# Decay attention and softplus feed-forward: scores of four jobs of batch 0 in two one-pass products, with a new plan

## The chip, the cores and the metric

The kernel runs on one core of one Trainium2 chip. The metric is the device time of one execution in microseconds, median of three. A profile of one execution shows what each engine did: TensorE (PE, its weight loads PEld), VectorE (DVE), ScalarE (ACT), GpSimd (POOL), and SyncE (SP), whose queue issues nearly all transfers.

## The reference

```python
def attn(q, k, v, f):                      # 8 batches, 8 heads, S = 576, D = 64
    scores = q @ k.T / 8                   # per batch and head
    cum = cumsum(log(clip(f, 1e-4, 1)))
    scores = where(causal, -1e9, scores + cum[:, None] - cum[None, :])
    p = exp(scores - max(scores)); p /= p.sum() + 1e-9
    return p @ v
x = attn(...).reshape(4608, 512)           # heads side by side
h = x @ w_in                               # 512 -> 2048
return (relu(h) + log1p(exp(-abs(h)))) @ w_out   # softplus, 2048 -> 512
```

The weights come in 64-bit floating point and are turned into 32-bit on the chip; all else is 32-bit.

## The kernel before, in words

**Two kinds of product.** TensorE multiplies 32-bit operands either in full precision, in several passes (the trace has two records for each such product), or in one pass with operands rounded to a shorter form (`F32R`). For the second kind each operand is split into a high and a low part, and the partial products are added up in PSUM. In the attention jobs of batches 1 to 7 the score of a query tile is made of two one-pass products (L1007, L1008): the first has 128 rows, q's high part over q's low part against k's high part twice; the second has 68 rows, with k's low part and, in four rows more, the sums of the decay. For that, q and k are loaded into both halves of the partitions ("raw" buffers, two of them), cast and subtracted into a tile `T` (two buffers, four planes of 576) by `prepare` (L933 to L978), and the decay's rows come by transfer from a table in DRAM.

**Batch 0** is taken apart, so that feed-forward work can begin early. Jobs 0 and 1 (`first`) do the first 128 queries of four heads each, jobs 2 to 5 (`second`) the next 128 of two heads each, jobs 6 to 13 (`rest`) the last 320 queries, 256 to 575, of one head each, in tiles of 64, 128 and 128 queries with 320, 448 and twice 288 keys. All fourteen are "plain": their scores are one full-precision product (L1002) over 64 rows of q and k and two rows of decay, laid straight into two tiles `T0` (which later become `T`) by one transfer of 288 KB and one small one. Their weights (p) stay 32-bit; they are turned over by transposes on TensorE (L1149) against an identity, or one with its halves exchanged (`halves`), copied from PSUM and multiplied with v (L1227). Jobs from 14 on are batches 1 to 7, one head each, 56 jobs.

**Feed-forward.** Two blocks of 128 tokens (tokens 0 to 255) run in full precision (L1516 up, L1630 down) between jobs 2 and 17 or so, as the weights come in: 32 pieces of 512 KB, each scaled, clipped and joined from its halves by ScalarE, VectorE and GpSimd (`load_f64`, L657 is the join). Later blocks use one-pass products with split weights (L1537, L1611), and the last tokens run in a scheme with fewer products (L2081, L2418).

**What sets the order.** All work is first written down as operations with the engines each may run on, a cost, and what it waits for. A planner (`Plan.run`, L229 on) then simulates the engines with those costs and emits, time after time, the operation with the earliest planned start less a bonus. Each engine executes its operations in the emitted order. Two tables steer it: `SOONER` holds the bonus in microseconds by kind of operation (a negative one holds it back), `RATHER` a bias by kind and engine. SP is one of the planned engines; a transfer occupies it for its size at 262 KB a microsecond, at least 0.6 us. Until the first feed-forward accumulation, wherever the plan has a gap on TensorE it emits filling products (128x128, L2673), 0.215 us each in the plan:

```python
elif clock["PE"] and op.start - clock["PE"] > 0.15:
    self.fill(engines["PE"], 0.1 + 0.7 * (op.start - clock["PE"]))
```

The plain jobs load three jobs ahead, those from 14 on two jobs ahead (L2684).

Of the kernel before, what the change touches and what calls it, by code (L numbers as in the profile page):

```python
# [32 lines left out]
PLAIN = 0  # L33
# [5 lines left out]
POOLB = -9.0  # L39
# [12 lines left out]
    "attention.finish.shift": 0.24,  # L52
    "attention.finish_stats.over early": 0.11,
    "attention.finish_stats.scale": -0.2,
    "attention.load.k": 2.33,
    "attention.load.q early": 0.41,
    "attention.load_quad.<lambda> early": 0.34,
    "attention.load_v.v": 0.78,
    "attention.load_v.v early": 0.01,
    "attention.output_tiled.put early": -0.08,  # L60
    "attention.split_v.v_hi early": -0.44,
    "attention.split_v.v_lo": 4.86,
    "attention.stat_tile.row_min": -0.1,
    "attention.stat_tile.shift": 0.18,
    "attention.stat_tile.shift early": 0.2,
    "attention.stat_tile.weight": 0.01,
    "attention.stat_tile.weight early": 0.1,
    "attention.weights.hi_part": 0.18,
    "attention.weights.lo_part": 0.16,
    "attention.weights.spread early": -0.35,  # L70
    "decay.load early": 4.01,
    "decay.log early": -4,
    "decay.store early": -0.24,
    "ffn_block.gate.hi_part": -0.21,
    "ffn_block.gate.lo_part": -0.11,
    "ffn_block.gate.raw": -0.03,
    "ffn_block.gate.raw early": -0.1,
    "ffn_block.second.load": 1.24,
    "ffn_block.split_stored.hi_part": -1.36,
    "ffn_block.split_stored.load": 1.24,  # L80
    "ffn_block.up_part.load": 0.64,
    "joined.row": 0.27,
    "load_f64.load early": 0.09,
    "load_f64.low early": -0.71,
    "load_f64.scale early": -0.02,
    "load_f64.sign early": 2.89,
    "mark": 4.55,
    "mark early": 2.26,
    "put_out.<lambda>": -0.05,
    "put_out.begin": 0.83,  # L90
    "set_rows.begin": -0.02,
    "split_w_in.hi_part": -0.12,
    "split_w_in.hi_part early": 0.11,
    "split_w_in.keep": -0.29,
    "split_w_in.keep early": -0.24,
    "split_w_in.lo_part": -0.24,
    "split_w_in.lo_part early": -0.21,
    "split_w_out.hi_part": 0.15,
    "split_w_out.hi_part early": 0.12,
    "store_x.store": -0.35,  # L100
    "super_blocks.down_set.split.low": 0.1,
    "super_blocks.down_set.sum_.<lambda>": 0.03,
    "super_blocks.gate.raw": -0.1,
    "super_blocks.lay_sums.<lambda>": 0.03,
    "super_blocks.lay_sums.low": 0.2,
    "super_blocks.lay_w.<lambda>": 5.14,
    "super_blocks.lay_w.load": 0.81,
    "super_blocks.lay_w.raw": 0.31,
    "super_blocks.lay_w.split.lo": 0.25,
    "super_blocks.lay_w.step.go": 0.16,  # L110
    "super_blocks.lay_x.less.go": 0.45,
    "super_blocks.lay_x.load": 0.05,
    "super_blocks.lay_x.split.high": -0.07,
    "super_blocks.lay_x.split.low": 3.71,
    "super_blocks.super_block.product.mm": -1.04,
    "super_blocks.super_block.ups.sum_of.go": -0.06,
    "turn_mask.turn": 0.1,
}
RATHER = {
    ("attention.finish_stats.scale", "ACT"): 0.18,  # L120
    ("attention.finish_stats.scale", "POOL"): -0.9,
    ("attention.prepare.<lambda>", "DVE"): 1.23,
    ("attention.split_v.v_hi", "ACT"): -0.33,
    ("attention.weights.hi_part", "DVE"): 1.46,
    ("attention.weights.keep early", "DVE"): 2,
    ("ffn_block.gate.lo_part", "DVE"): 1.97,
    ("ffn_block.gate.lo_part", "POOL"): -0.87,
# [227 lines left out]
def tile_decay_attention_softplus_ffn(  # L355
# [18 lines left out]
    B, D, H, _, S = qkT.shape  # L374
# [67 lines left out]
    T = {}  # L442
# [356 lines left out]
    def attention(job):  # L799
# [33 lines left out]
        def load_v(pairs=(None,)):  # L833
            for h in pairs:
# [21 lines left out]
                if h is not None:  # L856
                    more = 128, 1
# [1941 lines left out]
```

## Time and profile before

| | |
|---|---|
| median of three runs (lowest, highest) | 1119.87 us (1119.56, 1120.15) |
| the profiled execution | 1120.35 us |
| its span, first to last instruction | 1118.5 us |
| TensorE busy (weight loads) | 1103.4 us, 99% (955.1, 85%) |
| VectorE, ScalarE, GpSimd busy | 828.2, 822.2, 526.2 us (74%, 74%, 47%) |
| mean granted TensorE clock | 0.994 of full speed |
| moved by DMA | 200.5 MB, 179 GB/s |

Busy time of TensorE counts overlapping products from the start of the first to the end of the last; the distance between two starts tells what a product costs. The stretch to about 36 us is start-up, 36 to 160 us holds the rest of batch 0, the full-precision feed-forward and the first jobs of batch 1, and from there to about 800 us attention and feed-forward run side by side.

### The profile page before, as it was taken

Reading aid. Unit: us, or ns where it says so; the run is one execution under the profiler, and the core shown is the slowest. Engines: PE = TensorE matmul, PEld = TensorE weight load, DVE = VectorE, ACT = ScalarE, POOL = GpSimd, SP = SyncE. Lnnn points to the kernel's source line nnn. Section 1 sums busy time; section 2 is a strip of 40 time slices with the busy share of each in tenths; the row PEclk is TensorE's granted clock in tenths of the full one; section 3 lists DMA queues with packets and bytes.
Section 4 is the critical chain, followed back from the end, with each engine's and each line's share of the span. In section 5 each row is a group of like instructions: output and inputs, shape, how many; then the busy total and the mean of one; then the engine's idle time right before and its main releaser. Section 6 shows DMA issues by size and latency. Waiting matters only on the chain.

```text
span 1118.5 us, 21664 instructions
## 1 busy us (share of the span) xinstructions
PE 1103.4 (99%) x6766; PEld 955.1 (85%) x6766; DVE 828.2 (74%) x2378; ACT 822.2 (74%) x2017; POOL 526.2 (47%) x490
## 2 busy tenths in 40 slices
PE   9999999999999999999999999999999999999998
PEld 7787779888888888888888888888888788999998
DVE  4887887876676666676666866767765997998884
ACT  5898898978787898889898888787554766544431
POOL 2333687856664777746766566663010135001000
PEclk7999999999999999999999999999999999999999
DMA  7777666645446656565545755645686786443441
GB/s 195 225 224 234 213 193 203 208 153 169 147 156 193 196 166 200 165 189 168 180 151 160 233 167 172 194 140 153 213 242 199 232 222 192 149 122 122 148 123 58
DMA packets 163522, 200.54 MB, mean 179 GB/s; under 512 B 21872, under 2 KB 124560, under 8 KB 163408
## 3 DMA queue, kind: packets, MB, share of 16 engines
q1 hardware_dynamic: 163384, 199.15, 58.8%
q8 instruction: 53, 0.87, 0.3%
q14 instruction: 61, 0.50, 0.2%
q10 hardware_dynamic: 24, 0.02, 0.0%
HBM read 141.17 MB, written 57.84 MB: 178 GB/s over the span
## 4 chain that ended last, share of the span: by engine, by line
PE 85%; DVE 5%; ACT 4%; DMA 4%; issue 1%; POOL 0%; SPq 0%; ACTq 0%; DVEq 0%; POOLq 0%
PE acc L1611 17%; PE h L1537 15%; PE b L1149 8%; PE late_E L2418 7%; PE o L1296 6%; PE late_E L2081 5%; PE s L1007 3%; PE s L1008 3%; PE h L1516 2%; PE s L1002 2%; PE late_C L2081 2%; PE late_D L2081 2%; PE late_A L2081 2%; PE late_B L2418 2%; PE late_C L2418 2%; PE late_A L2418 2%
## 5 line engine op out<-in xcount | busy, mean ns | idle before, releaser
L1012 DVE CUSTOM_DVE_ANT_0 s<-s,cmask 128x288 f32<-128x288 f32 (+6 forms) x320 | 138.3, 437 | 64.4 <-PE s L1008 32.7
L1056 ACT ACTIVATE pb<-s,negm 128x288 f32<-128x288 f32 (+5 forms) x272 | 143.4, 530 | 46.6 <-DVE negm L1049 42.7
L1171 DVE TENSOR_TENSOR pl<-b,ph 128x512 fp32r<-128x512 f32 x168 | 106.8, 665 | 43.5 <-ACT ph L351 42.3
L351 ACT CAST ph<-b 64x128 fp32r<-64x128 f32 x224 | 102.5, 492 | 24.3 <-PE b L1149 22.9
L1581 POOL TENSOR_TENSOR gl<-e,gh 128x512 fp32r<-128x512 f32 x72 | 92.6, 1290 | 57.9 <-DVE gh L351 38.0
L962 POOL TENSOR_TENSOR T<-k,T 64x576 fp32r<-64x576 f32 x56 | 80.5, 1437 | 62.8 <-ACT T L351 29.2
L1007 PE MATMUL s<-T 128*128 128x192 f32 (+1 forms) x336 | 99.0, 302 | 2.2 <-ACT p L1056 2.0
L1008 PE MATMUL s<-T 68*128 68x192 f32 (+1 forms) x336 | 97.7, 295 | 0.0
L960 POOL TENSOR_TENSOR T<-q,T 64x576 fp32r<-64x576 f32 x56 | 80.3, 1434 | 25.6 <-ACT T L351 22.7
L1086 POOL TENSOR_SCALAR pb<-pb,rsum 128x320 f32<-128x320 f32 (+2 forms) x66 | 91.3, 1384 | 0.5
L1537 PE MATMUL h<-xh,wl 128*128 128x512 f32 (+1 forms) x320 | 91.2, 375 | 0.0
L1296 PE MATMUL o<-ph,vhl 128*128 128x512 f32 x336 | 88.2, 300 | 0.0
L1537 PE MATMUL h<-xh,wih 128*128 128x512 f32 (+1 forms) x320 | 81.4, 376 | 0.0
L1537 PE MATMUL h<-xl,wih 128*128 128x512 f32 (+1 forms) x320 | 79.5, 370 | 0.0
L1149 PE MATMUL b<-halves,pb 128*128 128x128 f32 x512 | 79.3, 273 | 0.0
L351 ACT CAST T<-k 128x576 fp32r<-128x576 f32 x112 | 74.9, 674 | 1.6 <-DMA k<-in_qkT 0.7
L1007 PEld LDWEIGHTS s<-T 128*128 128x128 f32 (+1 forms) x336 | 60.7, 181 | 13.3 <-ACT p L1056 4.5
L1611 PE MATMUL acc<-woh_dt_float32r,gh 128*128 128x512 f32 x176 | 71.4, 405 | 0.0
L924 POOL TENSOR_TENSOR vhl<-vr,vhl 128x384 fp32r<-128x384 f32 x56 | 57.3, 1023 | 28.2 <-ACT vhl L351 19.2
L1296 PE MATMUL o<-pl,vhl 128*128 128x512 f32 x224 | 68.9, 343 | 1.4 <-DVE pl L1171 1.3
L1611 PE MATMUL acc<-woh_dt_float32r,gl 128*128 128x512 f32 x176 | 69.2, 393 | 0.0
L1008 PEld LDWEIGHTS s<-T 68*128 68x128 f32 (+1 forms) x336 | 60.4, 180 | 10.2 <-issue 1.9
(743 smaller groups left out, 3360.2 us busy)
## 6 DMA issues: line engine op xcount, KB each, us to landing
wl<-wil_d SPq DMA_DIRECT2D x40, 512.0 KB
raw_d<-e SPq DMA_DIRECT2D x64, 256.0 KB
q<-in_qkT SPq DMA_DIRECT2D x112, 144.0 KB
k<-in_qkT SPq DMA_DIRECT2D x112, 144.0 KB
vr<-in_vR SPq DMA_DIRECT2D x64, 160.0 KB
x_d<-x SPq DMA_DIRECT2D x28, 288.0 KB
g_d<-gh SPq DMA_DIRECT2D x56, 128.0 KB
g_d<-gl SPq DMA_DIRECT2D x56, 128.0 KB
```

The source lines that it names most:

```text
L351: (e.tensor_copy if hasattr(e, "tensor_copy") else e.copy)(out, in_)
L1007: e.matmul(o, qA[:, S - end : S - q0], kA[:, a:z], start=True, stop=False)
L1008: e.matmul(o, qB[0:ST, S - end : S - q0], kB[0:ST, a:z], start=False, stop=True)
L1012: e.tensor_tensor_reduce(out=box["o"], in0=box["o"], in1=cmask[0:n_q, right - w : right], scale=-0.125, scalar=m0 if i else 3.0e38, op0=AL ...
L1056: e.activation(o, box["o"], AF.Softplus, bias=m1, scale=-1.0, accum_out=acc)
L1149: e.transpose(box["ps"][0 : x.shape[1], at : at + one.shape[1]], x, one)
L1171: e.tensor_sub(box["l"], box["ps"][:, 0:w], box["h"].bitcast(F32))
L1296: e.matmul(boxes[gi]["ps"][0:m, a:z], st["vhl"][:, c, 0:m], pbox[which][:, o : o + z - a], start=gi in fresh and which == "h", stop=gi == ...
L1537: e.matmul(o, l, r, start=m == 0, stop=m == 11)
L1611: e.matmul(st["acc", tt], l, r[fc], start=first and m == 0, stop=last and m == 2,)
L2081: e.matmul(banks[to], stationary(x, j), at(b, y, j), start=start and m == 0, stop=m == 5, skip_group_check=not start,)
L2418: e.matmul(like(o, y), x, y, start=q == 0 and f_ == 0 and m == 0, stop=q == NQ - 1 and f_ == 1 and m == 2,)
```

## The change

Four of the eight `rest` jobs (6 to 9) stay as they were. The other four (10 to 13, heads 4 to 7) take their scores as the jobs from 14 on do, in two one-pass products out of `T`: q's last 320 columns and all of k are loaded twice, cast and subtracted by `prepare`, and the decay's rows come from DRAM. Their v stays 32-bit, as do their weights; since their queries now lie in reversed blocks of 64, some transposes use a 68-wide identity. `T`'s fixed rows are cleared for jobs 10 and 11 in place of 14 and 15. The transfers of the first q/k and v are costed at 410 and 220 KB in place of 256 and 128, the filling rule has other numbers, and both tables are new.

```diff
-PLAIN = 0
+HYB = 4
...
-    "attention.load_quad.<lambda> early": 0.34,
+    "attention.load_quad.<lambda> early": 3.4,
...
-    "decay.load early": 4.01,
-    "decay.log early": -4,
+    "decay.clip early": 5.27,
+    "decay.load early": 5.68,
...
-                elif clock["PE"] and op.start - clock["PE"] > 0.15:
-                    self.fill(engines["PE"], 0.1 + 0.7 * (op.start - clock["PE"]))
+                elif clock["PE"] and op.start - clock["PE"] > 0.1:
+                    self.fill(engines["PE"], 0.15 + 0.9 * (op.start - clock["PE"]))
...
+        first32 = number < nfirst + HYB
...
-                    more = 128, 1
+                    more = 220, 1
...
-                add_dma(lambda e, h=h: qk(e, h), 256, after=[o])
+                add_dma(lambda e, h=h: qk(e, h), 410, after=[o])
...
-                    e.dma_start(out=st["q"][r : r + 64], in_=qkT[b, :, heads[0], 0])
+                    e.dma_start(out=st["q"][r : r + 64, 0 : S - qs], in_=qkT[b, :, heads[0], 0, qs:])
...
-            split_v()
-            if number < nplain + 2:
-                set_rows(number % 2, T0_end[2 * (number % 2)] + T0_end[2 * (number % 2) + 1])
+            if not plain:
+                split_v()
+            if number < nfirst + HYB + 2:
+                set_rows(number % 2, T0_end[number % 2])
...
-                    if plain:
+                    if first32:
                         e.matmul(
                             o, part32(0, q0, q0 + P), part32(1, a, z), start=True, stop=not quad,
                         )
                         return
...
-                        second = q0 < lo and ti < nt - 1
+                        second = q0 < lo and (ti < nt - 1 or plain and not first32)
...
+                            x, less = pt[pi][:, c : c + P], second or n_q == 64
+                            blocks.append((x[0:68], at, ident[0:68, 0:68]) if less else (x, at, halves))
...
-                (load32 if plain else load)()
+                (load32 if first32 else load)()
...
-            load=loads, prepare=None if plain else prepare, fin=finish_stats,
+            load=loads, prepare=None if first32 else prepare, fin=finish_stats,
...
-                if m >= nfirst and (m < nplain) == (m == n + 3) and m < len(jobs):
+                if m >= nfirst and (m < nfirst + HYB) == (m == n + 3) and m < len(jobs):
```

## Rows read from the trace of the kernel before

**Rows 1.** The page, busy time of TensorE and its granted clock in 40 slices of the span, in tenths.

```profile
PE 1103.4 (99%) x6766; PEld 955.1 (85%) x6766; DVE 828.2 (74%) x2378; ACT 822.2 (74%) x2017; POOL 526.2 (47%) x490
...
PEclk7999999999999999999999999999999999999999
```

**Rows 2.** Busy time of each engine by stretch. Columns: stretch, its length, busy us of PE, PEld, DVE, ACT and POOL with instructions, granted clock as a share, DMA share, GB/s.

```profile
11.79:25.45 13.66, 13.66 (x60) 10.82 (x58) 6.25 (x29) 7.35 (x24) 3.95 (x8) 0.50 0.62 225
...
60.00:116.00 56.00, 55.70 (x393) 43.16 (x392) 42.83 (x120) 48.66 (x109) 19.24 (x24) 1.00 0.79 240
...
160.00:1100.00 940.00, 933.18 (x5618) 818.88 (x5619) 703.12 (x1981) 691.42 (x1697) 453.47 (x393) 1.00 0.58 176
```

**Rows 3.** The chain that ended last, in order of time, of the first 60 us: start, us, what.

```profile
3.38 6.38 DMA T<-in_qkT
9.83 0.64 ACTq L887
10.53 0.47 ACT pb L1056 x2
...
23.34 1.28 PE fill L2673 x6
24.62 0.87 PE s L1002 x2
25.52 0.43 DVE s L1012
```

**Rows 4.** Instructions of TensorE in order of time: start, us, engine, line, operation. Full-precision scores of one `rest` job at 320, 448 and twice 288 columns, each with the row that comes next; two records make one product.

```profile
69.14 0.70 PE L1002 MATMUL s<-T 66*128 66x320 f32 x2
69.68 1.06 PE L1516 MATMUL h<-x,woh_dt_float 128*128 128x128 f32 x8
...
71.56 0.92 PE L1002 MATMUL s<-T 66*128 66x448 f32 x2
72.31 1.02 PE L1630 MATMUL acc<-wol_dt_float,g 128*128 128x512 f32 x2
...
74.58 1.14 PE L1002 MATMUL s<-T 66*128 66x288 f32 x4
75.55 1.02 PE L1630 MATMUL acc<-wol_dt_float,g 128*128 128x512 f32 x2
```

**Rows 5.** The same view, 124 to 133 us: the first of the two one-pass products of a piece (L1007) and the row after the second one (L1008 stands between, left out).

```profile
124.10 0.47 PE L1007 MATMUL s<-T 128*128 128x448 f32 x1
...
124.62 0.49 PE L1149 MATMUL b<-ident,pb 128*128 128x128 f32 x3
...
125.09 0.38 PE L1007 MATMUL s<-T 128*128 128x288 f32 x1
...
125.44 1.06 PE L1516 MATMUL h<-x,woh_dt_float 128*128 128x128 f32 x8
...
129.07 0.39 PE L1007 MATMUL s<-T 128*128 128x320 f32 x1
...
129.45 0.37 PE L1007 MATMUL s<-T 128*128 128x448 f32 x1
...
129.87 1.88 PE L1630 MATMUL acc<-wol_dt_float,g 128*128 128x512 f32 x4
...
131.86 0.30 PE L1007 MATMUL s<-T 128*128 128x288 f32 x1
...
132.13 1.88 PE L1630 MATMUL acc<-wol_dt_float,g 128*128 128x512 f32 x4
```

**Rows 6.** The same view: seven 128-wide transposes and the row after them, and two 68-wide ones and the row after them.

```profile
58.32 0.93 PE L1149 MATMUL b<-ident,pb 128*128 128x128 f32 x7
59.08 1.02 PE L1630 MATMUL acc<-wol_dt_float,g 128*128 128x512 f32 x2
...
137.25 0.29 PE L1149 MATMUL b<-ident,pb 68*128 68x68 f32 x2
137.37 0.49 PE L1149 MATMUL b<-halves,pb 128*128 128x128 f32 x3
```

**Rows 7.** Groups of instructions by line and shape, 60 to 160 us: busy us, mean ns, idle time before. The splitting of q and k for the first jobs of batch 1.

```profile
L960 POOL TENSOR_TENSOR T<-q,T 64x576 fp32r<-64x576 f32 x5 | 7.2, 1435 | 5.2 <-ACT T L351 5.2
...
L351 ACT CAST T<-q 128x576 fp32r<-128x576 f32 x6 | 4.0, 672 | 0.0
...
L351 ACT CAST T<-k 64x576 fp32r<-64x576 f32 x5 | 3.4, 675 | 0.0
```

**Rows 8.** What the SP queue waited for from 60 to 116 us: us in total, times, longest. L907 issues q's loads, L912 k's.

```profile
SPq L907 <- POOL T L960: 2.1, 1, 2.1
SPq L912 <- POOL T L962: 1.6, 1, 1.6
```

**Rows 9.** Instructions of VectorE in order of time: the join of a piece of w_in.

```profile
105.81 0.69 DVE L657 SCALAR_TENSOR_TENSOR woh_dt_float<-ti,woh_dt_float 128x512 uint32<-128x512 uint32 x1 [0.92 <-ACT woh_dt_float L651]
```

**Rows 10.** Instructions of TensorE in order of time: the next up products after it.

```profile
106.72 1.06 PE L1516 MATMUL h<-x,woh_dt_float 128*128 128x128 f32 x8
```

**Rows 11.** Groups of TensorE instructions by line, whole span: the filling products.

```profile
L2673 PE MATMUL fill<-cmask 128*128 128x128 f32 x46 | 8.2, 315 | 0.0
```

**Rows 12.** Who waited for whom in the first 40 us: us in total, times, longest. VectorE's row minima waiting for scores.

```profile
DVE s L1012 <- PE s L1021: 5.2, 5, 2.0
DVE s L1012 <- PE s L1002: 3.8, 3, 2.1
```

More of the change, by code (lines that the diff above doesn't have):

```diff
@@ L77 @@
[L77 to L83, printed above, removed]
-    "load_f64.low early": -0.71,
[L85 to L101, printed above, removed]
+    "attention.finish.put": 0.1,
+    "attention.finish.shift": 0.33,
+    "attention.finish_stats.scale": -0.19,
+    "attention.load.k early": 4.14,
+    "attention.load.q early": 0.61,
@@ new lines @@
+    "attention.stat_tile.weight early": 0.09,
+    "attention.weights.hi_part": 0.11,
+    "attention.weights.keep early": 0.02,
+    "attention.weights.lo_part": 0.14,
+    "attention.weights.spread early": -0.4,
+    "attention.weights.turn": 0.19,
+    "decay.clip early": 5.27,
+    "decay.load early": 5.68,
+    "decay.split early": -0.42,
+    "decay.store early": -0.11,
+    "ffn_block.down_part.mm early": -0.16,
+    "ffn_block.gate.hi_part": -0.22,
+    "ffn_block.gate.keep": -0.68,
+    "ffn_block.gate.lo_part": 0.22,
@@ new lines @@
+    "ffn_block.gate.raw": -0.01,
+    "ffn_block.gate.raw early": -0.23,
+    "ffn_block.second.load": 1.06,
+    "ffn_block.split_stored.load": 3.26,
+    "ffn_block.split_x.hi_part": 0.53,
+    "ffn_block.split_x.lo_part": 0.41,
+    "joined.row": 0.07,
+    "load_f64.low early": -0.71,
+    "load_f64.scale early": -0.08,
+    "load_f64.sign early": 4.04,
+    "mark early": 3.61,
+    "put_out.<lambda>": -0.07,
+    "set_rows.begin early": -4,
+    "split_w_in.hi_part": -0.14,
+    "split_w_in.hi_part early": 0.28,
@@ L116 @@
-    "super_blocks.super_block.ups.sum_of.go": -0.06,
-    "turn_mask.turn": 0.1,
+    "super_blocks.lay_sums.high": -0.3,
+    "super_blocks.lay_sums.low": 0.71,
+    "super_blocks.lay_w.<lambda>": 4.97,
+    "super_blocks.lay_w.load": 0.09,
+    "super_blocks.lay_w.split.hi": -0.22,
+    "super_blocks.lay_w.split.lo": 0.63,
+    "super_blocks.lay_w.step.go": 0.41,
+    "super_blocks.lay_x.less.go": 0.69,
+    "super_blocks.lay_x.load": 2.02,
+    "super_blocks.lay_x.split.low": 2.96,
+    "super_blocks.super_block.product.mm": -0.84,
@@ L118 @@
+    "super_blocks.super_block.ups.moved.<lambda>": -0.27,
+    "super_blocks.super_block.ups.sum_of.go": 3.6,
+    "turn_mask.turn early": -0.15,
 }
 RATHER = {
[L120 to L126, printed above, removed]
@@ L145 @@
+    ("super_blocks.lay_w.split.hi", "DVE"): -0.2,
+    ("super_blocks.lay_w.split.lo", "DVE"): 0.37,
+    ("super_blocks.lay_w.step.go", "DVE"): 0.18,
+    ("super_blocks.lay_w.step.go", "POOL"): 0.54,
+    ("super_blocks.lay_x.less.go", "DVE"): -2,
+    ("turn_mask.turn early", "ACT"): -1.15,
 }
```

146 lines of the change are left out of this document (75 added, 71 removed).

## The prediction

> **What bounds the kernel now.** I read the page's busy line and slices first: TensorE is busy for 99% of the span, and its granted clock is full in all but the first slice [rows 1]. The table of stretches comes next [rows 2]. From 60 to 116 us, where the four touched jobs and most of the full-precision feed-forward work lie, TensorE is busy 55.70 of 56 us, ScalarE 48.66, VectorE 42.83 and GpSimd only 19.24. From 160 to 1100 us TensorE idles 940 - 933.18 = 6.8 us in all. So TensorE's own queue is the bound from about 36 us on, and time taken off it there moves everything behind it, as long as no other engine overtakes it. Before that the kernel is bound otherwise: from 11.79 to 25.45 us the granted clock is 0.50, the lower of the two levels (1.2 against 2.4 GHz), and the chain of waits runs from the fourth q/k transfer through the ScalarE queue into TensorE [rows 2, 3].
>
> **Scores of four jobs.** I price a product by the distance between starts in the PE timeline, since durations overlap. In full precision the pieces of one job take 69.68 - 69.14 = 0.54 us (320 columns), 0.75 (448) and 0.97 (two of 288), 2.26 us in all [rows 4]. Two one-pass products of the same widths, as the first job of batch 1 makes them among the same neighbours, take 0.38 (320), 0.52 and 0.42 (448), 0.35 and 0.27 (288) [rows 5]. With the means this is 0.38 + 0.47 + 2 x 0.31 = 1.47 us, a saving of 0.79 us a job and 3.2 us for four. With the dearest pieces it is 0.38 + 0.52 + 0.70 = 1.60 (2.6 us saved), with the cheapest 0.38 + 0.42 + 0.54 = 1.34 (3.7 us). I take -3.2: the means come from the same mix of neighbours.
>
> **Transposes.** With queries in reversed blocks of 64, 5 of a job's 12 weight blocks (three of the 64-query tile, one diagonal block of each other tile) are turned by a 68-wide identity in place of a 128-wide one. Seven 128-wide ones take 59.08 - 58.32 = 0.76 us, 0.109 each; two 68-wide ones 0.12, 0.06 each [rows 6]. 20 x 0.05 = -1.0 us. Nothing speaks for less than -0.8 or more than -1.2.
>
> **Added splitting.** Each of the four jobs now casts q, k and a second half of k and subtracts twice. A cast of 128x576 took 0.67 us on ScalarE, one of k's 64x576 0.675, a 64x576 subtraction 1.43 us on GpSimd [rows 7]; q is only 320 wide, so I scale its two by 320/576 (estimate): 0.67 + 0.675 + 0.37 = 1.7 us of casts and 1.43 + 0.8 = 2.2 us of subtractions a job, 6.9 and 8.9 us for four. The two clearings of T's extra rows only move to an earlier job. GpSimd has 36.8 us free in 60 to 116 us, VectorE 13.2 and ScalarE 7.3, so I put the term at 0: the cover is that slack, and the casts may go to VectorE. If all the casts go to ScalarE and none to VectorE, ScalarE needs 48.66 + 6.9 = 55.6 us in a stretch that should shrink to 51.8: +3.8, the upper bound.
>
> The Trainium skill (Trace Analysis, section Identifying the Most-Contended Engine) says that matmul busy time is no good measure of how close TensorE is to its limit and that the busy share of weight loads is better. By the weight loads TensorE would have a quarter left in this stretch (43.16 of 56 us [rows 2]); the first two terms would bring nothing and the sum would be +0.6, close to the rival below in which ScalarE gives the gain back. The starts in rows 4 to 6 follow each other without a hole, which is why I don't take it.
>
> **Transfers.** Each of the four jobs loads q and k twice (2 x 80 and 2 x 144 KB by the code) in place of one 288 KB transfer: 160 KB more, 0.6 MB in all, 2.7 us of transfer at the stretch's 240 GB/s, beside work. With the rows of decay it is four more issues on SP's queue per job, each q/k issue behind a wait for a free "raw" buffer. What stands behind such a wait on SP is a weight load, and SP waited 2.1 and 1.6 us once each for q's and k's buffers [rows 8]. The weights have little lead at one place: the last word of a w_in piece was joined by VectorE at 105.81 + 0.69 = 106.50 us and TensorE's next product with those weights began at 106.72 [rows 9, 10]. I take 0, since the loads of the four jobs go out two jobs ahead, in the same way as from job 14 on, and TensorE has scores of the next jobs to put first; the upper bound is one longest wait a job, 4 x 2.1 = +8.4.
>
> **The start.** Three edits act here. Filling products are now planned from 0.1 us of gap instead of 0.15, with 0.15 + 0.9 x gap instead of 0.1 + 0.7 x gap: by the formula a stretch that had one gets two, three become four, five become seven. The 23 of today (46 records, two to a product [rows 11]) become some 34. At half clock one takes 1.28 / 3 = 0.43 us, at full clock half of that. In the stretch at 23.34 us they are on the path: VectorE's next minimum at 25.52 waits for the score behind them [rows 3]; one more there and one before it is 0.9, those after 25 us stand beside VectorE, which was busy. From 0 (all in gaps that are there anyway) to 11 x 0.43 = +4.7; I take +0.6. The first transfers cost the plan more, and the tables let the decay's logarithm go early and the decay rows ahead of the V loads. On the chip the fourth q/k transfer lands at 3.38 + 6.38 = 9.76 us and the ScalarE queue, which issues rows behind it, holds the first softplus until 10.53 [rows 3]. If the V loads (4 x 128 KB) delayed it, moving them is worth up to 0.51 MB at 225 GB/s, -2.3 us; they were issued after it, so I take 0.
>
> The Trainium skill (DMA: Bandwidth & Descriptors, section Queues, rings and completion order) says that on each DMA engine a queue's descriptors are taken in the order of the ring. By that rule V loads issued later on the same queue could not have held up the fourth transfer, and the term is 0; without it the sum would be 2.3 us lower.
>
> **Tables.** The order of the other 940 us is drawn anew. Its idle time is 6.8 us [rows 2]; taking half of it away or adding half as much gives -3.4 to +3.4, value 0.
>
> **Sum.** -3.2 - 1.0 + 0 + 0 + 0.6 + 0 = -3.6 us on the profiled execution's 1120.35, 1116.75. That execution was 0.48 above the median of the three, so in terms of the median 1116.3. What can be told from no change is 0.2%, 2.24 us: faster means below 1117.63, slower above 1122.11.
>
> **Rivals.**
> *The clock stays up.* The 0.5 stretch follows a time in which TensorE stood idle until its fifth score. If more filling keeps the clock at its upper level, the products between 11.79 and 25.45 us take half. VectorE waited 5.2 + 3.8 = 9.0 us for scores in the first 40 us [rows 12]; a third of this, 3 us, is what I let the path gain beyond the forecast: 1113.3. For: the filling formula. Against: the idle time before the drop comes from the ScalarE queue's hold until 10.53, which the plan, where these rows do not wait for the fourth transfer, does not see. Chance 0.20.
> *Given back by ScalarE.* The casts all on ScalarE: +3.8, 1120.1. For: the casts of batch 1's jobs seen in rows 7 all ran there. Against: VectorE is a choice for each. Chance 0.19.
> *The weights come late, and it is slower.* The q/k loads of jobs 10 to 13 stand on SP before the last weight loads and wait for buffers; feed-forward products wait in TensorE's in-order queue with the next jobs' scores behind them. Price up to 8.4: 1124.7. It decides from 3.6 us of lateness on, and makes the kernel slower by the bound from 5.8 on. For: the 0.2 us of lead in rows 9 and 10. Against: it is one place, and the planner sees these waits. Chance 0.12.
> The forecast itself has 0.43, with its own range 1114.5 to 1118; the rest, 0.06, is for the tables going wrong or right by more than that.
>
> **Chances.** Faster: 0.39 of the forecast's 0.43, the clock's 0.20, 0.02 of ScalarE's and 0.03 of the rest, 0.64. Within 0.2%: 0.04, 0.15 and 0.01, 0.20. Slower: the weights' 0.12, 0.02 of ScalarE's and 0.02 of the rest, 0.16. The range 1111.5 to 1121.5 reaches over the clock and ScalarE cases and leaves out most of the weights' case.
>
> **What would show it.** Right: from 60 us to the end of the last batch-0 job, L1002 has half its calls fewer among the 320, 448 and 288 wide ones, about 16 pairs of L1007 and L1008 take their place at 0.27 to 0.52 us a piece, 20 transposes turn 68-wide, and the first product of batch 1 comes some 3.5 us sooner. Wrong: TensorE waits for joined weights or for casts of T between 60 and 120 us; the granted clock's lower stretch is longer or gone; the idle time from 160 us on changes by more than 3 us.

## The result, and the profile after

The changed kernel took **1131.83 us** (median of four, 1129.95 to 1133.52) beside 1119.71 for the kernel before in the same runs (1117.33 to 1120.15): ratio 1.0122, 95% interval 1.0094 to 1.0151. Slower by some 12 us, well beyond the 0.2% that can be told, where 3.6 us less was predicted. The profiled execution took 1131.47, its span 1129.7.

The page of the changed kernel, busy time and granted clock:

```profile
PE 1103.1 (98%) x6796; PEld 956.4 (85%) x6796; DVE 855.8 (76%) x2364; ACT 822.1 (73%) x2028; POOL 565.5 (50%) x513
...
PEclk9999999999999999999999999999999999899999
```

TensorE was busy as long as before (1103.4 [rows 1]), so the 11.2 us that the span grew show as idle time of TensorE: 1129.7 - 1103.1 = 26.6 us against 1118.5 - 1103.4 = 15.1. That the busy time did not fall, though the scores became cheaper, has two reasons that rows show: 2.6 us more of filling products (10.8 for 8.2 [rows 11]), and waits that lie inside the busy time (under *Scores* below). Where the idle time lies is read from stretches, first of the kernel before, then of the changed one (stretch, length, PE, PEld, DVE, ACT, POOL busy, granted clock, DMA share, GB/s):

```profile
80.00:100.00 20.00, 19.70 (x139) 14.89 (x139) 14.85 (x43) 14.55 (x36) 4.69 (x7) 1.00 0.82 242
100.00:160.00 60.00, 59.52 (x391) 45.41 (x389) 48.15 (x153) 55.23 (x140) 41.15 (x39) 1.00 0.66 207
900.00:1000.00 100.00, 98.51 (x614) 88.85 (x614) 91.55 (x193) 57.52 (x117) 27.60 (x28) 1.00 0.60 176
```

```profile
11.79:25.45 13.66, 13.66 (x113) 11.35 (x113) 10.10 (x49) 10.61 (x34) 4.10 (x8) 1.00 0.66 231
60.00:116.00 56.00, 54.51 (x356) 38.23 (x354) 39.65 (x114) 48.12 (x110) 27.90 (x32) 1.00 0.65 194
80.00:100.00 20.00, 19.72 (x139) 15.39 (x139) 9.88 (x29) 15.88 (x36) 10.49 (x11) 1.00 0.62 188
100.00:160.00 60.00, 53.34 (x343) 39.68 (x344) 48.93 (x145) 50.48 (x126) 39.56 (x36) 0.94 0.61 184
900.00:1000.00 100.00, 96.03 (x551) 85.46 (x550) 90.40 (x190) 55.52 (x114) 26.34 (x23) 0.97 0.59 174
118.53:121.94 3.41, 3.41 (x17) 3.41 (x17) 1.52 (x3) 3.41 (x8) 2.81 (x2) 0.50 0.75 247
142.42:145.83 3.41, 2.91 (x7) 1.79 (x8) 2.19 (x7) 2.33 (x5) 3.25 (x3) 0.50 0.54 181
961.62:968.45 6.83, 6.05 (x28) 6.05 (x29) 6.83 (x17) 4.46 (x10) 0.00 (x0) 0.50 0.24 79
```

Between 100 and 160 us TensorE idles 60 - 53.34 = 6.66 us where it idled 0.48, and between 900 and 1000 us 3.97 where it idled 1.49: 8.7 of the 11.5 us of added idle time. The half clock moved rather than grew: 13.66 us at the start before [rows 2], now 3.41 + 3.41 + 6.83 = 13.65 us after the new idle times. VectorE shows what precedes the first loss: 9.88 us of work between 80 and 100 us instead of 14.85. In the order of TensorE's instructions the last full-precision score comes at 71.3 us (job 9) and the first one-pass score at 85.1 (job 10); before, these two neighbours were job 13 at 116.1 and job 14 at 118.3. For 14 us no job has scores, and the softmax engines run short of work.

What TensorE waited for in the changed kernel, in 100 to 160 us and in 940 to 980 us, and last in 940 to 980 us of the kernel before:

```profile
PE b L1175 <- DVE ph L1195: 1.4, 1, 1.4
PE s L1029 <- DVE pl L1198: 1.2, 1, 1.2
PE s L1029 <- ACT pb L1078: 0.9, 3, 0.5
PE s L1029 <- DVE x L1278: 0.7, 2, 0.4
```

```profile
PE late_B L2445 <- DVE late_raw L2412: 2.3, 1, 2.3
PE late_E L2445 <- DVE late_w L2412: 1.0, 1, 1.0
PE late_E L2108 <- DVE late_xh L2035: 0.6, 1, 0.6
```

```profile
PE late_E L2418 <- DVE late_T L2385: 1.0, 1, 1.0
PE late_B L2418 <- DVE late_raw L2385: 0.3, 1, 0.3
```

And the changed kernel's chain of waits (start, us, what) through the hand-over to T:

```profile
74.30 2.65 DMA aug_d<-ch
77.01 0.51 SPq L922
77.58 3.45 DMA q<-in_qkT
81.11 0.46 ACT T L365
...
83.03 1.41 POOL T L980
84.46 0.47 SPq L927
84.97 0.60 SPq L927
85.61 5.19 DMA sto<-in_w_out
90.82 0.68 ACT to L646
```

It reads like the rival of the late weights: the store of the decay sums, the load of q, casts, a subtraction on GpSimd, and a weight load that stands on SP behind the next job's k load (L927). Weight pieces 22 to 31 did issue 1.6 us (piece 22, 80.4 for 78.8) to 13.3 us (piece 31, 128.1 for 114.8) later. Whether that is the cause is what the runs had to tell. Four theories: the added loads or their place on SP (LOADS, SP, HAND-OVER), the added splitting (CASTS), the clock (CLOCK), and the order in which the new plan lays the work into each engine's queue (ORDER).

### The profile page after: what moved, and what is told of

Same layout as the page of the kernel before. It is cut to its first block, busy times and chain, and to the rows that moved or that the text cites. A ratio compares the mean times of both kernels' runs of the same rounds, so it can differ in the third digit from the quotient of the medians.

```text
span 1129.7 us, 21812 instructions
## 1 busy us (share of the span) xinstructions
PE 1103.1 (98%) x6796; PEld 956.4 (85%) x6796; DVE 855.8 (76%) x2364; ACT 822.1 (73%) x2028; POOL 565.5 (50%) x513
## 4 chain that ended last, share of the span: by engine, by line
PE 84%; DVE 8%; ACT 4%; DMA 2%; issue 1%; POOL 0%; SPq 0%; DVEq 0%; ACTq 0%; POOLq 0%
PE h L1564 17%; PE acc L1638 15%; PE b L1175 7%; PE late_E L2445 7%; PE o L1323 6%; PE late_E L2108 6%; PE s L1030 3%; PE s L1029 3%; PE late_A L2445 2%; PE late_B L2445 2%; PE late_C L2445 2%; PE late_D L2108 2%; PE late_C L2108 2%; PE late_D L2445 2%; PE late_A L2108 2%; PE h L1543 1%
## 5 line engine op out<-in xcount | busy, mean ns | idle before, releaser
L1034 DVE CUSTOM_DVE_ANT_0 s<-s,cmask 128x448 f32<-128x448 f32 (+6 forms) x320 | 138.1, 436 | 63.1 <-PE b L1175 37.4
L980 POOL TENSOR_TENSOR T<-k,T 64x576 fp32r<-64x576 f32 x60 | 85.8, 1430 | 127.1 <-ACT T L365 70.7
L365 ACT CAST ph<-b 128x448 fp32r<-128x448 f32 (+1 forms) x222 | 101.3, 491 | 24.4 <-PE b L1175 23.8
L1109 POOL TENSOR_SCALAR pb<-pb,rsum 128x320 f32<-128x320 f32 (+2 forms) x87 | 115.7, 1335 | 2.6 <-DVE rsum L1092 2.6
L1029 PE MATMUL s<-T 128*128 128x448 f32 (+4 forms) x352 | 105.1, 304 | 4.9 <-ACT pb L1078 1.2
L1030 PE MATMUL s<-T 68*128 68x448 f32 (+4 forms) x352 | 102.7, 296 | 0.0
L978 POOL TENSOR_TENSOR T<-q,T 64x576 fp32r<-64x576 f32 (+1 forms) x60 | 84.5, 1409 | 18.8 <-ACT T L365 15.2
L365 ACT CAST T<-k 128x576 fp32r<-128x576 f32 x120 | 80.5, 673 | 3.1 <-DMA k<-in_qkT 1.4
L1323 PEld LDWEIGHTS o<-ph,vhl 128*128 128x128 f32 x336 | 63.9, 190 | 8.4 <-ACT p L1078 0.9
L1638 PE MATMUL acc<-wol_dt_float32r,gh 128*128 128x512 f32 x176 | 69.0, 392 | 0.0
```

What stands on the lines that cost most here:

```text
L365: (e.tensor_copy if hasattr(e, "tensor_copy") else e.copy)(out, in_)
L1029: e.matmul(o, qA[:, S - end : S - q0], kA[:, a:z], start=True, stop=False)
L1030: e.matmul(o, qB[0:ST, S - end : S - q0], kB[0:ST, a:z], start=False, stop=True)
L1034: e.tensor_tensor_reduce(out=box["o"], in0=box["o"], in1=cmask[0:n_q, right - w : right], scale=-0.125, scalar=m0 if i else 3.0e38, op0=AL ...
L1109: e.tensor_scalar(a, a, f_, None, ALU.mult)
L1323: e.matmul(boxes[gi]["ps"][0:m, a:z], st["vhl"][:, c, 0:m], pbox[which][:, o : o + z - a], start=gi in fresh and which == "h", stop=gi == ...
```

## Experiments

Each ratio, with its 95% interval, is to the kernel before measured beside it; the changed kernel stands at 1.0122, and at 1.0121 [1.0088, 1.0155] when run again.

### The loads, their queue and the casts, in the changed kernel's order

The q and k loads of jobs 10 to 13 by another engine:

```diff
             def q(e):
+                e = nc.gpsimd if plain else e
...
             def k(e):
+                e = nc.gpsimd if plain else e
```

> The changed kernel with one edit: the q and k loads of jobs 10 to 13 (L922, L927) are issued by GpSimd instead of SP, at the same place of the order; no other instruction moves. Theory SP (the added q and k loads hold the weight loads up in SP's queue, so feed-forward work comes late and TensorE idles between 100 and 160 us): weight pieces 24 to 31 issue several us earlier than in the changed kernel (there 91.5 to 128.1 us), TensorE's idle time in 100 to 160 us (6.65 us) at least halves, and the time falls by 4 to 10 us, to 1122 to 1128. Theory ORDER (the order written for each engine already puts the feed-forward work late, the wait on SP is only its echo): the weights issue earlier but the time moves by less than 2 us. Theory CASTS (the splitting added on ScalarE and GpSimd is what holds): no gain, or up to 3 us slower, because GpSimd now also issues 16 transfers.

Measured 1.0134 [1.0107, 1.0161]; TensorE idles 60 - 52.88 = 7.1 us in 100 to 160 us. The weights did not come forward: piece 22 issued at 82.5 us, piece 31 at 131.4. With the q and k loads gone, SP waited with a V load (L863) for TensorE's output, and for the buffers of the weights themselves, which GpSimd and ScalarE release (66 to 125 us):

```profile
SPq L863 <- PE o L1256: 9.7, 3, 6.0
SPq L642 <- POOL wol_dt_float L660: 8.8, 4, 3.1
SPq L642 <- ACT to L646: 5.1, 2, 4.5
```

That the q and k loads hold SP up falls; whether late weights matter at all is left to the next runs. The Trainium skill (Trainium Kernel Development and Optimization, section Key Constraints) says that transfers issued from SP, ScalarE and GpSimd run on the same DMA engines, and that issuing from several engines saves issue time only. This run fits that, without showing the sharing: less issuing on SP brought nothing.

The store and the first loads earlier (the plan is made as before and written into a list; one move is made in it; then it is emitted):

```diff
-            op.emit(engines.get(eng))
+            seq.append((op, op.emit, eng))
...
+    first = [store] + [u for u in store.users if kind_of(u.emit) == "mark"]
+    first += [o for o in ops if kind_of(o.emit) in ("attention.load.q", "attention.load.k")][:2]
+    for op in first:
+        seq = hoist(plan, seq, op, at)
```

> The changed kernel with three transfers moved up in SP's order and nothing else: the store of the decay sums (in the changed kernel at 74.3 us) and the q and k loads of job 10 (77.0 and 78.3 us) go to about 50 us. Theory HAND-OVER (between the last fp32 scores at 71.3 us and the first one-pass scores at 85.1 us no job has scores, because the store and the first loads come late; the engines drain and this is paid back later): the gap of 13.8 us shrinks to under 8 us, VectorE's 9.88 us of work in 80 to 100 us rises, and the time falls by 3 to 8 us. Theory ORDER: TensorE has feed-forward products ahead of job 10's scores in its order (82.8 to 94 us), so the scores hardly move and the time changes by less than 2 us. Theory SP: the moved loads only push other loads back; no gain.

Measured 1.0145 [1.0120, 1.0170]. The first load issued at 57.4 us, not at about 50, but the first one-pass score came at 89.5, 13.8 us after the last full-precision one, a gap as long as in the changed kernel: TensorE's queue has feed-forward products there. The first weight load behind the moved transfers went back from 54.4 to 59.9 us, and in 60 to 80 us TensorE lost 2.64 us. The hand-over is not held by its loads alone. Nor does the gap decide the time: it is 2.8 us in rate_300 below, which is slower still, and 11.6 us in order_both, which is faster.

No waiting for loads at all. The ten weight pieces, then the q and k of jobs 10 to 13, then both (the diff of the first; the second reads `wih[:, 1, 0:S]` likewise):

```diff
         def load(e):
...
+            if at >= 22:
+                e.dma_start(out=box["s"][:, 0:8], in_=src[:, 0:8])
+                box["s"] = wih[:, 0, 0:1024].bitcast(U32).rearrange("p (c t) -> p c t", t=2)
+                return
             e.dma_start(out=box["s"], in_=src)
```

> The changed kernel, every engine's order untouched; weight pieces 22 to 31 (in the changed kernel issued at 80.4 to 128.1 us) are loaded as 8 of 512 columns only, and their conversion reads a weight tile that has long been there, so that it waits for no load. Left out: the contents of these ten pieces. Theory LOADS (the ten loads come late and everything behind them with them): joins of pieces 22 to 31, at 88.3 to 155.7 us in the changed kernel, come several us earlier, TensorE's idle time in 100 to 160 us (6.65 us) falls below 3, and the time falls by 4 us or more. Theory ORDER (ScalarE, VectorE and GpSimd reach these conversions late because of what stands ahead of them in their own order): the joins move by less than 2 us, and so does the time.

> The changed kernel, every engine's order untouched; the q and k loads of jobs 10 to 13 move 8 columns each into their buffers, and the casts read a weight tile that has long been there, so that they wait for no load. Left out: the scores of jobs 10 to 13 have other data. Theory LOADS OF Q AND K (3.45 us and 2.55 us of these transfers stand in the chain of waits at 77.6 and 98.1 us): the first one-pass scores (85.1 us) and the following jobs come 2 to 5 us earlier and the time falls by 3 us or more. Theory ORDER: less than 2 us.

> The edits of the two loads runs together: neither the conversions of weight pieces 22 to 31 nor the casts of jobs 10 to 13 wait for a load, every engine's order untouched. Left out: the contents of these ten pieces, and the q and k of these jobs. Theory LOADS, of either kind: the time falls by the sum of the two runs, 6 us or more, and TensorE's idle time in 100 to 160 us is nearly gone. Theory ORDER: the time stays within 3 us of the changed kernel, TensorE still idles 4 us or more between 100 and 160 us, waiting for VectorE and ScalarE.

Measured 1.0119 [1.0091, 1.0147], 1.0117 [1.0086, 1.0148] and 1.0112 [1.0085, 1.0139]. The last one in 100 to 160 us, and its waits from 95 to 165:

```profile
100.00:160.00 60.00, 53.54 (x363) 40.58 (x362) 51.71 (x156) 51.80 (x130) 41.98 (x38) 0.97 0.44 133
```

```profile
PE b L1185 <- DVE ph L1205: 1.4, 2, 1.2
PE b L1185 <- ACT pb L1088: 1.2, 3, 0.6
PE s L1039 <- DVE p L365: 1.2, 2, 0.7
PE s L1039 <- DVE pl L1208: 1.1, 1, 1.1
```

The DMA share fell from 0.61 to 0.44 and TensorE still idles 6.5 us, waiting for VectorE and ScalarE. In this order no load holds the kernel (the intervals alone would leave room for some 3 us, the idle time that stays does not): LOADS falls, and with it the reading of the chain above. A chain shows what came last at each step; shorten that step and another stands in its place.

Half of the added splitting left out:

```diff
             def high(e, i, x, rows):
-                if x == "q":
+                if nfirst + HYB + 1 < number < nplain:
+                    copy(e, t[rows, i, 0:8], st[x][rows, 0:8])
+                elif x == "q":
```

(and the same in `less`).

> The changed kernel, every engine's order untouched; for jobs 12 and 13 the three casts and two subtractions of the preparation work on 8 columns instead of 320 or 576. Left out: the split of q and k of these two jobs. That is about half of the added splitting: 2 x (0.46 + 0.68 + 0.30) us of ScalarE and 2 x (1.41 + 0.8) us of GpSimd. Theory CASTS (the added splitting on ScalarE and GpSimd is what the 100 to 160 us stretch pays for): the time falls by 2 to 4 us. Theory ORDER or LOADS: less than 1 us.

Measured 1.0113 [1.0092, 1.0135], idle time 60 - 54.15 = 5.85 us. At most a small part comes from this half. CASTS falls as far as this run reaches; the other half of the splitting was left in.

### Structure and plan apart

The structure with the tables, costs and filling of before (struct_only); the kernel before with the new tables alone (tables_only); and with the new filling alone (before_fill):

```diff
-    "decay.store early": -0.11,
+    "decay.store early": -0.24,
...
-                add_dma(lambda e, h=h: qk(e, h), 410, after=[o])
+                add_dma(lambda e, h=h: qk(e, h), 256, after=[o])
```

(struct_only, from the changed kernel, every entry of both tables so; tables_only exchanges the entries the other way in the kernel before and nothing else; before_fill:)

```diff
-                elif clock["PE"] and op.start - clock["PE"] > 0.15:
-                    self.fill(engines["PE"], 0.1 + 0.7 * (op.start - clock["PE"]))
+                elif clock["PE"] and op.start - clock["PE"] > 0.1:
+                    self.fill(engines["PE"], 0.15 + 0.9 * (op.start - clock["PE"]))
```

> Only the structural part of the change: jobs 10 to 13 in one-pass products out of T, with the tables, the transfer costs and the filling of the kernel before. Theory SP (each one-pass job brings six issues on SP where an fp32 job has two): slower than the kernel before by 8 us or more, and the new tables of the change gave part of that back. Theory TABLES (the new entries are what costs, the structure is worth its 4 us): within 3 us of the kernel before, or faster.

> The kernel before with the two tables of the change and nothing else: all eight jobs of the last 320 queries in fp32, no added loads, casts or rows. Theory ORDER (new entries lay the work out for the new structure; the old structure loses by them): 5 to 12 us slower than before, with weight pieces 24 to 31 later than the kernel before has them (86.1 to 114.8 us) although no added q and k load stands ahead of them. Theory STRUCTURE (the added steps are what costs): within 2 us of before. It also shows the 4 to 5 us around 950 to 970 us if these come from the entries of the last stage.

> The kernel before with the filling of the change alone (a gap from 0.1 us on is filled, with 0.15 + 0.9 of it); its order is the same. What it tells: the part of the start-up. If the clock at the start is what counts, the half-clock stretch from 11.79 to 25.45 us shortens and the time falls by 1 to 3 us; if the start-up waits for data anyway, no change beyond 1 us.

Measured 1.0434 [1.0407, 1.0462], 1.0114 [1.0077, 1.0150] and 1.0001 [0.9976, 1.0025]. struct_only, then the changed kernel, from 80 to 160 us:

```profile
80.00:160.00 80.00, 63.92 (x373) 47.29 (x372) 58.38 (x167) 54.30 (x132) 38.60 (x34) 0.81 0.60 182
```

```profile
80.00:160.00 80.00, 73.06 (x481) 55.07 (x481) 58.81 (x174) 66.37 (x160) 50.06 (x47) 0.96 0.61 185
```

With the old tables the structure idles TensorE 16 us in this stretch, and weight pieces 28 to 31 issue at 150 to 168 us. The new tables repair most of that. In tables_only they cost the old structure as much as the whole change costs, though it has none of the added steps; its weights come partly earlier (piece 24 at 82.6 us for 86.1), partly later (piece 28 at 108.4 for 100.5). That the two sums agree is chance: tables_only idles TensorE 3.5 us in 100 to 160 us where the changed kernel idles 6.7, and 10.0 us in 200 to 900 us where it idles 4.5 (the kernel before 5.1). The tables choose engines as well as places (GpSimd is busy 550.9 us in tables_only, 526.2 before), so this run does not show the order alone. The waits of tables_only around 950 us are the changed kernel's:

```profile
PE late_B L2432 <- DVE late_raw L2399: 2.3, 1, 2.3
PE late_E L2432 <- DVE late_w L2399: 1.0, 1, 1.0
PE late_E L2095 <- DVE late_xh L2022: 0.6, 1, 0.6
```

So these waits of the last stage come with the new entries, not with the structure. The filling is worth nothing that can be measured.

### The order alone

One constant of the planner, RATE, which is what a transfer is counted at and changes no transfer:

```diff
-RATE = 262
+RATE = 300
```

> The changed kernel with one constant of its planner other (RATE, the KB per us that it counts for a transfer, 300 in place of 262): the same instructions, loads and sizes, laid out in another order over the whole kernel; nothing is taken away. Theory ORDER: the time moves by far more than the 4 us that the change was to bring, 10 us or more slower, since the entries of the tables fit one set of costs only; TensorE idles more in 80 to 160 us. Theory WORK: what there is to do sets the time, and it stays within 4 us of the changed kernel.

Measured 1.0262 [1.0228, 1.0296], 1.4% or some 15 us over the changed kernel with the same work; a few steps change their engine too (GpSimd has 506 instructions for 513). From 80 to 160 us:

```profile
80.00:160.00 80.00, 65.06 (x392) 47.57 (x390) 58.89 (x160) 61.73 (x144) 31.74 (x32) 0.87 0.65 199
```

TensorE idles 80 - 65.06 = 14.9 us (the changed kernel 6.9), and its granted clock is 0.87 (0.96): 80 x 0.09 = 7.2 us of full clock less, nearly as much as the 8.0 us of added idle time.

Then the order itself: single instructions and short blocks are shifted inside each engine's queue, and a shift is kept where by the planner's own costs the stretch ends sooner. Engines, loads and sizes stay, and the buffers change hands in the same turns. order_moved shifts between about 45 and 175 us, after_tail between 890 and 975 us, order_both in both places, and before_moved treats the kernel before in the same way.

```diff
+ORDER = {
...
+}
...
+    for first, new in ORDER.items():
+        ops[first : first + len(new)] = [place[at] for at in new]
```

> The changed kernel, same instructions on the same engines and same loads; only the order in which they stand on each engine between about 45 and 175 us is moved, by small steps inside what the buffers' turns allow. Theory ORDER (what the changed kernel loses in 100 to 166 us comes from where the work stands in the engines' queues, no load and no single cast holds it): TensorE's idle time in 100 to 160 us (6.65 us) falls to 4.5 us or less and the time falls by 2 to 4 us. Theory WORK (ScalarE and VectorE have too much to do in this stretch, whatever the order): no change beyond 1 us.

> The changed kernel with the moves between 890 and 975 us alone. Theory TABLES (the new entries of the last stage cost it 4 to 5 us around 950 to 970 us, as the run tables_only has the same three waits of 2.3, 1.0 and 0.6 us): TensorE's idle time in 900 to 1000 us falls from 3.97 us to under 1.5 us, no half-clock stretch is left there, and the time falls by 3 to 5 us. Theory VECTORE (it has too much to do at this place, whatever the order): less than 1 us.

> The changed kernel, same instructions, engines and loads; the order on each engine moved by small steps between about 40 and 240 us (as in the run order_moved, which brought 0.4%) and between 890 and 975 us. Theory ORDER (the 103 to 166 us stretch and the last stage lose by where the work stands in the queues): both repairs add up, TensorE idles under 4.5 us in 100 to 160 us and under 1.5 us in 900 to 1000 us (3.97 us in the changed kernel), and the time comes to within 0.4% of the kernel before, some 8 us under the changed kernel. Theory WORK: it stays at the 0.8% of order_moved.

> The kernel before with the same kind of small moves, between 40 and 240 us and between 740 and 990 us. It tells whether such moves repair what the change did to the order or would help any kernel: if the order before is close to what such steps can reach, the time falls by less than 2 us; by 4 us or more if the moves are a gain of their own, and then the repaired new structure has to be held against this kernel and not against the kernel before.

> The changed kernel as it is, once more beside the others of this call: 1.2% over the kernel before, as first measured. All theories say the same; it is the reference for the two repaired versions on this chip.

Measured: order_moved 1.0081 [1.0049, 1.0113]; after_tail 1.0064 [1.0044, 1.0085]; order_both 1.0038 [1.0019, 1.0057]; before_moved 1.0017 [0.9998, 1.0037]; after_again 1.0121. order_both by stretches:

```profile
80.00:100.00 20.00, 20.00 (x141) 15.70 (x140) 14.47 (x39) 18.28 (x42) 11.38 (x11) 1.00 0.67 197
...
100.00:160.00 60.00, 55.81 (x387) 42.06 (x385) 49.06 (x153) 50.85 (x131) 37.94 (x36) 0.97 0.63 194
...
900.00:1000.00 100.00, 100.00 (x615) 90.13 (x614) 94.72 (x206) 56.40 (x119) 29.39 (x26) 1.00 0.61 183
```

TensorE's idle time in 900 to 1000 us is gone (3.97 to 0), that in 100 to 160 us fell from 6.66 to 4.19, and VectorE has its 14.47 us of work between 80 and 100 us back. With nothing but places in queues changed, 1.0121 - 1.0038 = 0.83% came back, 8.5 us between the medians (1130.75 and 1122.23). The same treatment gave the kernel before nothing. ORDER stands for this part.

The part is uneven. The shifts in the last stage alone brought 6.8 us (after_tail, median 1123.99), and more than what the change had lost there: from the first product of the last stage (L2081, later L2108) to the end the kernel before takes 325.3 us in its profile, the changed kernel run again 326.4 (first profiled, with its half-clock stretch, 329.0) and order_both 322.4. The shifts in 40 to 240 us brought the other 1.8 us, and the intervals of after_tail and order_both overlap. At one granted clock they brought nothing that shows: at 0.998 three executions of after_tail took 1122.06 to 1123.77 us and five of order_both 1122.43 to 1125.68. What these shifts did was to leave fewer stretches at half clock (order_both 0.998 to 1.000, after_tail 0.995 to 0.998).

The largest shifts, by the places in the two profiles, are these; no run takes one of them by itself. In 40 to 240 us the store of the decay sums went 15 places forward on SP and a V load that waits for TensorE's output 26 back; on VectorE two casts of weight pieces went 60 and 65 places back and low halves of weight pieces mostly 17 to 50 back. In the last stage low halves of the summed weights (`wih`, L2317 in the changed kernel) went some 30 places back on VectorE and sums for the down products 14 to 22 forward. The changed kernel's chain has `wih` between the operands (`late_w`, `late_raw`) that TensorE waits for:

```profile
958.06 0.67 DVE fX L2378 x2
958.73 0.16 DVE late_w L2412
...
958.99 0.41 DVE wih L2317
...
961.75 0.61 DVE late_raw L2412
...
962.40 1.22 PE late_B L2445 x4
```

### The clock, and the remainder

Products that keep TensorE busy in the two waits at 958 and 960 us:

```diff
+                        for _ in range({"P1": 9, "P5": 19}.get(p, 0) if first and f_ == 0 else 0):
+                            e.matmul(like(o, bh), ah, bh, start=True, stop=True)
                         for m, (x, y) in enumerate(((ah, bh), (ah, bl), (al, bh))):
```

> The changed kernel with 28 repeats of two products put in where TensorE waits at 957.8 and 959.9 us (9 and 19 repeats of the first product of a group, which start=True overwrites, so the sum is the same); no other instruction moves. Theory CLOCK (of the 4 to 5 us lost around 960 us most is the stretch 961.6 to 968.4 us at half clock that follows the idle time): the stretch is granted the full clock and the time falls by 2 to 3.4 us. Theory VECTORE (what is lost there is VectorE's lateness, products at half clock are hidden behind it): the time stays within 1 us of the changed kernel.

Measured 1.0103 [1.0073, 1.0134]: the stretch 961.62 to 968.45 is granted the full clock in the profile, but the interval overlaps the changed kernel's. And after_again had no half clock there either, with the same 3.98 us of idle time and 1.0121. Inconclusive for the size. Over the whole kernel the clock is not what makes the change slower: six executions of after_again were granted 0.992 to 0.997, and those of the kernel before beside them 0.990 to 1.000, mostly 0.993 to 0.995.

What order_both leaves was looked for in the loads and in the joins of ten weight pieces on VectorE:

```diff
         def join(e):
             x, t = box["x"].bitcast(U32), box["t"].bitcast(U32)
+            if at >= 22:
+                x, t = x[:, 0:8], t[:, 0:8]
```

> The order of order_both (0.38% over the kernel before), and the conversions of weight pieces 22 to 31 and the casts of jobs 10 to 13 wait for no load, as in no_wqk. Left out: the contents of these ten pieces and the q and k of these jobs. Theory LOADS (with the order mended, the added loads hold the remainder): the time falls by 3 us or more against order_both, to the kernel before or under it. Theory CHAIN (the remainder, like the part that is mended, is the chain from TensorE's scores over VectorE and ScalarE back to TensorE): it stays within 2 us of order_both.

> The order of order_both with the joins of weight pieces 22 to 31 on VectorE working on 8 of 512 columns (ten times about 0.5 us less of VectorE between 88 and 156 us). Left out: the contents of these ten pieces. Theory CHAIN (TensorE waits in 100 to 160 us for VectorE, whose queue holds weight work between the steps of the softmax): the time falls by 1.5 to 4 us against order_both. Theory LOADS: less than 1 us.

Measured 1.0037 [1.0019, 1.0055] and 1.0042 [1.0022, 1.0063]: both as order_both. Neither the loads nor this part of VectorE's work holds what remains.

## Why the prediction was wrong

*Tables: "value 0", -3.4 to +3.4.* This is the step that failed. It let the new order shift only the 6.8 us of idle time from 160 us on by half, up or down. The new tables alone cost 1.14% (tables_only, 12.7 us of 1117.0), and mending places in the queues gave 8.5 us back. Two things were wrong in the step. It left out what lies before 160 us, where the prediction took TensorE's own queue for the bound (55.70 of 56 us busy [rows 2]); that it was busy was a property of one order, not of the work. From 160 to 1100 us the idle time did grow by only 3.1 us, to 9.9, inside the range of the step, with 6.83 us at half clock behind it; the 6.2 us added in 100 to 160 us stand in no term. And it took bounds from idle time that is there, though an order can add far more: RATE alone added some 15 us, the structure in the old tables 4.34% or 48.

*Scores: -3.2, and transposes: -1.0.* Right in kind. Of the 16 pieces of jobs 10 to 13, 11 follow at 0.35 to 0.50 us; the other five stand 0.67 to 0.74 apart, three of them with their second product over 0.3 us late and no releaser named, so that a job takes 1.95 us with these waits in it, and not 1.47: 1.2 us saved on four jobs instead of 3.2. A pair of 68-wide transposes takes 0.12 us, as priced:

```profile
97.37 0.28 PE L1175 MATMUL b<-ident,pb 68*128 68x68 f32 x2
97.49 0.50 PE L1175 MATMUL b<-halves,pb 128*128 128x128 f32 x3
```

The gain went into waiting. The Trainium skill (Perfetto Trace Analysis, section Identifying the Most-Contended Engine) would read TensorE's limit from the share of weight loads, 38.23 of 56 us here in 60 to 116 us and 43.16 before [rows 2]. The rival that the prediction drew from it, that the two terms bring nothing, agrees with the times so far; it does not agree with the rows of the products, which did close up, and it tells of no loss.

*Added splitting: 0.* Right as a term. The casts all ran on ScalarE, the case feared, and ScalarE did not overflow (48.12 us in 60 to 116, 48.66 before); leaving half of them out (thin_prep) changed nothing that can be told.

*Transfers: 0, "TensorE has scores of the next jobs to put first".* The value stands, as no_wqk shows, but the reason was wrong: from 71.3 to 85.1 us there were no scores to put first. The slower rival got its outward sign, weights up to 13.3 us late behind q and k loads, and still was not the cause. Its place was the right stretch; its mechanism fell in no_wload and no_wqk.

*The start: +0.6.* The filling grew from 46 records [rows 11] to 76, 38 products where 34 were expected:

```profile
L2700 PE MATMUL fill<-cmask 128*128 128x128 f32 x76 | 10.8, 280 | 0.0
```

The half clock was gone from the start as in the rival "the clock stays up". But the filling is no gain (1.0001), and the start of tables_only has the full clock with the old filling. With the new tables TensorE's first products, the warming ones, start at 4.91 us (1.04 before) and the first score comes at 9.87 (5.77 before; tables_only 10.10); from there on TensorE works without the hole that the kernel before has ahead of 11.04 us. The first feed-forward accumulation comes at 40.86 us instead of 42.47, so the start came out some 1.6 us ahead (an estimate from these two rows); in before_fill, profiled with its clock up, it comes at 36.23. The hold until 10.53 us that the prediction speaks of is on the first softmax step, not on a softplus.

*What would show it.* "TensorE waits ... for casts of T between 60 and 120 us" was looked for in the wrong queue: it waited for steps of the softmax, and from 100 us on. One sign of being right came nearly as told, the first product of batch 1 at 115.65 us instead of 118.27, 2.6 us sooner, and the kernel was slower all the same. The idle time from 160 us on changed by 3.1 us, which the prediction names as a sign of being wrong.

What stays open is more than the last 0.4% of order_both. That figure compares kernels at different granted clocks: the kernel before runs mostly at 0.993 to 0.995, with its half-clock start, order_both at 0.998 to 1.000. At 1.000 six executions of order_both took 1120.26 to 1124.14 us and two of the kernel before, measured beside them, 1111.97 and 1112.50: some 9 us, 0.8%. The 0.2% to before_moved (1.0017) has the same fault; its one execution at 1.000 took 1115.59. What is lost lies ahead of the last stage, which begins at 795.63 us in order_moved and at 786.30 in before_fill, both profiled at full clock or nearly (1.000 and 0.999). No run shows what holds it. It is not the loads, not the joins of ten weight pieces, and not the half of the splitting that was left out; that another order would bring it back, with the 4 us that the products save, is not shown, and no version here beats the kernel before.

## What to carry to other kernels

Where one planner lays out all queues, an edit that shifts its costs redraws everything; price the order as a term of its own, with the spread that a harmless change of a constant gives, before adding up what instructions cost. Full TensorE in the trace of before does not bound what another order can lose. To tell order from work, run the new tables on the old structure and the new structure on the old tables, and take suspected waits away while each engine's order stands still: when nothing moves, those waits are not the cause. Then move places in the queues and nothing else. And compare versions at the same granted clock, or a remainder of 0.8% passes for 0.4%.

## What was not expected of the hardware

One kernel's executions differ by how long TensorE is granted its lower clock. The kernel before ran from 1111.97 to 1123.88 us in 29 executions; in another set of 14 its two with a mean granted clock of 1.000 took 1111.61 and 1112.33 us, and its three at 0.994 took 1118.62 to 1121.12. The half-clock stretch of rows 2 is thus not in every execution. In the changed kernel such a stretch follows idle time, so that idle time can cost about double (in rate_300 8.0 us of it came with 7.2 us of lower clock): from 115.12 to 116.83 us TensorE was busy 0.58 us, and from 118.53 on the granted clock was 0.50 although it was busy throughout.

```profile
115.12:116.83 1.71, 0.58 (x5) 0.42 (x4) 1.64 (x8) 1.30 (x4) 0.57 (x1) 1.00 0.65 183
116.83:118.53 1.70, 1.52 (x21) 1.09 (x20) 1.53 (x8) 1.44 (x7) 0.00 (x0) 1.00 0.74 149
118.53:120.24 1.71, 1.71 (x9) 1.71 (x9) 0.64 (x2) 1.71 (x5) 1.19 (x1) 0.50 0.71 268
```
